# A new order of the head and of all step plans in a fused pooling-attention and mixer kernel

## The chip, the cores and the metric

The kernel runs on one core of a Trainium2 chip. The metric is the device time of one execution, in microseconds, the median of three runs. A run is also profiled; "us" are microseconds from the start of the profiled span.

The core has five engines with a queue of instructions each: TensorE (PE) multiplies matrices, VectorE (DVE), ScalarE (ACT) and GpSimd (POOL) work on elements, SyncE (SP) issues transfers. POOL and ACT issue transfers too. An engine takes its instructions strictly in their order, so an instruction that waits holds up all that stand behind it.

## The reference

Batch 8, 8 heads, 576 rows, head dimension 64; everything comes and goes in float32.

```python
def _attn_ref(q, k, v):
    k_p = k.reshape(B, H, Sp, 8, D).mean(axis=3)      # Sp = 72
    v_p = v.reshape(B, H, Sp, 8, D).mean(axis=3)
    scores = scale * np.matmul(q, k_p.transpose(0, 1, 3, 2))
    attn = softmax(scores)
    return np.matmul(attn, v_p)

x = attn_out.transpose(0, 2, 1, 3).reshape(B, S, H * D)   # 8 x 576 x 512
def _moe_ref(x, w_tok1, w_tok2, w_ch1, w_ch2):
    h = np.maximum(x.transpose(0, 2, 1) @ w_tok1, 0.0) @ w_tok2   # 576 -> 256 -> 576
    u = x + h.transpose(0, 2, 1)
    h2 = np.maximum(u @ w_ch1, 0.0) @ w_ch2                       # 512 -> 1536 -> 512
    return u + h2
```

## The kernel before

**Steps.** The work of a batch is cut into small named steps, each a few instructions on several engines. `2.K0` is step K0 of batch 2. The names that matter here:

- `lk`, `lq`, `lv` (lines 118 to 131): load k, q or v of a batch to bfloat16. POOL issues these transfers; k and v take two each, q takes one. Each landing area has two buffers, so a load waits until the batch two before has been read.
- `K0`, `K1`, `V0`, `V1` (`pool8`, lines 171 to 180): POOL sums groups of eight rows of k or v, half of the heads each, in three additions (lines 174, 175 and 178 or 180). `v1` does the same on DVE. `kpT` (line 222): PE transposes the pooled keys, ACT copies them.
- `Q0`, `Q1` (line 284): DVE transposes the queries. `s0` to `s2` (lines 297 and 306): scores on PE, exponentials on ACT.
- `av0` to `av4` (lines 379 to 384): PE sums the values with their weights, DVE divides. `at0`, `at1` (lines 393, 395): product with w_tok1. `u0` to `u4` (lines 410 to 416): product with w_tok2 on PE, and the sum u = x + h on DVE.
- To give the mixer u with its rows and columns exchanged, batches 1 and 2 use `t0` to `t3` (PE transposes, line 424). From batch 3 on it goes through DRAM: `M0`, `M2`, `M4` write u there (line 434), `M` and `MT` read it back (line 446), both issued by SP, and `T0` to `T5` (line 458) transpose on DVE.

**Units.** The channel mixer of one batch is a unit (`unit_fast`, lines 574 on). Units 0 to 7 are the batches, unit 8 holds the last 64 rows of all batches together. A unit has 24 half tiles of the first product (line 517, ACT writes GT at line 521) and then seven products of 12 matmuls each (line 583), called x, y, z, x again, w, z again and x again; the last unit has no w and two more x. Seven products take the place of eight by sums of GT and of w_ch2 that DVE makes: `=1` to `=4` (lines 545 and 557) and, once, `w0` to `w3`. DVE adds the parts at line 626. A unit yields after each half tile and after every four matmuls of a product, 45 times; these are its slots, 0 to 44, some 0.43 us each.

**The order.** Nothing is scheduled by a program at build time. `HEAD` is the list of steps ahead of unit 0, the loads (`L...`) among them, and `PLAN[n]` says which steps follow which slot of unit n. The steps of batch n+1 and the loads and pooling of batches n+2 and n+3 are woven into unit n in this way. In HEAD, `d4` is four matmuls on zeros, `p0` and `p1` (line 159) permute w_tok2 on ACT and POOL, `kp`, `kt`, `q`, `o`, `e` pool, transpose and score batch 0, `a`, `m`, `X`, `A` are its weighted sums and its token mixer.

Each engine's queue gets the instructions in the order in which the steps stand, and each instruction waits for what it reads and for the buffers that it writes. Some of these waits are not visible in the plan:

- PSUM has four banks that go round (`take` and `give`, lines 81 to 88): a step takes the bank that has been free longest, and its first matmul waits until the bank's last reader is done. Scores and weighted sums share two larger buffers.
- `g` is a gate (lines 711 to 713): DVE sets a flag and POOL copies it, so that POOL's next work does not begin before DVE has come to this place; DVE's next gate waits for POOL's copy.
- At most eight of POOL's transfers are under way: the next one waits for the landing of the one eight before. POOL stands still meanwhile.

In the last unit (`last`), x is kept in two halves, and DVE adds in the order s1, the output addition of y, s5 of z, s of x, and then the outputs.

Of the kernel before, what the change touches and what calls it, by code (L numbers as in the profile page):

```python
# [17 lines left out]
SYNC = mybir.EngineType.SP  # L18


HEAD = """LkA LkT LkB LvT Lq LvA LvB Lt1 Lk1 Lt2 Lc1b Lc1a Lq1 Lc1c Lv1 Lc1d p1 Lc2a Lc2b Lc2c d2 d2 d3 d1 d4 d4 c0 c1 prep q0 kp0 kp1 kt0 q1 d1 o0 kt1 kp2 e0 e1 q3 kt2 o1 q2 e3 vpool0 o3 e2 a00 vpool1 a02 o2 m01 d1 d1 m00 a04 X1 m03 a14 m02 X0 m04 p0 a10 a12 1.kpool m10 m14 m12 m13 m11 A1 A0 X2 X3 A2 A3"""
PLAN = [
# [9 lines left out]
]  # L32


# [1 line left out]
def kernel(  # L36
# [49 lines left out]
    def give(t):  # L86
        i = next(i for i, h in enumerate(held) if h[0] is t)
        free.append(held.pop(i)[1])
# [421 lines left out]
    def chunk(u, c, a):  # L510
        return a[:, c::2] if "paired" in u else a[:, c * P:(c + 1) * P]
# [62 lines left out]
    def unit_fast(n, u):  # L574
        last = n == B
# [4 lines left out]
        def product(ps, a, w, start, after, split=False, end=None):  # L580
            for i in range(2):
                for m in range(NH):
                    nc.tensor.matmul(out=ps[i] if split else ps[:, i], lhsT=chunk(u, i, a(m)), rhs=w(m),  # L583
                                     start=start and m == 0 and (i == 0 or split), stop=(m == NH - 1),
                                     skip_group_check=True)
                    if (i * NH + m) % 4 == 3 and (i, m) != (1, NH - 1):
                        yield
                if split:
                    after(i)
            if not split:  # L590
                after(slice(0, 2))
            if end is not None:
                give(end)
            yield

        def bank(split=False):
            if split:
                return [ps_two.tile([P, 2, 512], FP32, name="p2")[:, 0, 0:256] for _ in range(2)]
            return take([P, 2, 256], FP32)

        def keep(name):
            return outp.tile([P, 2, 256], FP32, name=name, bufs=1)

        def residual(i, half):
            if "paired" in u:
                r = u["u"][:, i].rearrange("p (a k f) e -> p e k a f", a=4, k=4)[:, :, 2 * half:2 * half + 2]
            else:
                r = u["u"][:, i, half * 256:(half + 1) * 256].rearrange("p n e -> p e n")
            return lambda e: r[:, e]

        def cols_of(o, half):
            return lambda e: o[:, e, half * 256:(half + 1) * 256]

        def part(t):
            return (lambda e: t[e]) if type(t) is list else lambda e: t[:, e]

        def plus(out, ps, other, then=None):
            def go(e):
                if type(e) is slice and len(other(e).shape) > 3:
                    go(0)  # L620
                    go(1)
                    return
                aps = [f(e) for f in (out, ps, other)]
                if len(aps[2].shape) == 4:
                    aps[:2] = [x.rearrange("p (k a f) -> p k a f", k=2, a=4) for x in aps[:2]]
                nc.vector.tensor_tensor(out=aps[0], in0=aps[1], in1=aps[2], op=ALU.add)
                if then is not None:
                    then(e)
            return go

        def store_part(cols, engines):
            def go(i):
                if len(engines) == 2:
                    engines[i].dma_start(out=tail_rows(1, cols)[:, i], in_=ob[:, i, cols])
                elif i == 1:
# [4 lines left out]
        oa, ob = (outp.tile([P, 2, DM], FP32, name="o") for _ in range(2))  # L640
        x, y = bank(last), bank()
        s1 = keep("s1")
        yield from product(x, lambda m: GT[:, m, lo], lambda m: w_ch2[:, m, lo], True,
                           plus(part(s1), part(x), residual(0, 0)), last)
        yield from product(y, lambda m: GT[:, NH + m, lo], lambda m: w_ch2[:, NH + m, lo], True,
                           plus(cols_of(oa, 0), part(y), part(s1)), end=y)
        z = bank()
        s5 = keep("s5")
        yield from product(z, lambda m: SG[:, 0, m], lambda m: TW[:, 0, m], True,
                           plus(part(s5), part(z), residual(1, 1)))  # L650
        s2 = keep("s1")
        yield from product(x, lambda m: SG[:, 1, m], lambda m: TW[:, 1, m], False,
                           plus(part(s2), part(x), residual(0, 1)), last)
# [80 lines left out]
    with tc.manual_schedule(engines={PE, POOLE, DVE, ACT, SYNC}):  # L734
# [8 lines left out]
        for i in range(2):  # L743
            nc.vector.memset(values[i][:, :, D], float(POOL))
            nc.vector.memset(exps[i][:, H * S:], 0.0)
            nc.vector.memset(rests[i], 0.0)
        for i, s in enumerate(HEAD.split()):
            if i == 3:
# [34 lines left out]
```

## Time and profile before

| | us |
|---|---|
| median of three runs | 266.19 (266.13 to 266.20) |
| the profiled execution | 266.17 |
| its span | 264.4 |
| TensorE busy | 256.2 |
| VectorE busy | 178.4 |
| ScalarE busy | 119.6 |
| GpSimd busy | 153.1 |

A row of the timeline gives the start in us, the length in us, the engine, the line of the code, the operation, output and inputs with their shapes, and how often it follows itself; in brackets the idle time of the engine before it and what ended that. Rows of the waits give the engine and line that waited, for whom, and in all how long, how often and the longest. Rows of the groups give the total and the mean length in ns. The granted TensorE clock is 0.999 over the span.

### The profile page before, as it was taken

What the parts mean: (1) busy time and instruction counts of PE and PEld (TensorE: products, weight loads), DVE (VectorE), ACT (ScalarE), POOL (GpSimd) and SP (SyncE); (2) the same over time, 40 slices, a digit from 0 to 9 for tenths busy, and PEclk for the clock granted to TensorE, in tenths of its full rate; (3) what the DMA queues carried; (4) which work ended last, traced back from release to release, by engine and by line L of the source; (5) the groups of instructions that cost most, each with busy time, mean ns of one, the idle gap of its engine ahead of it and who ended that gap; (6) DMA issues with size and microseconds to landing.
All of it is one profiled execution on the core that took longest, in us unless ns stands there. A gap on an engine that the chain in (4) does not pass through costs nothing.

```text
span 264.4 us, 5328 instructions
## 1 busy us (share of the span) xinstructions
PE 256.2 (97%) x2121; PEld 160.3 (61%) x2121; DVE 178.4 (67%) x370; ACT 119.6 (45%) x195; POOL 153.1 (58%) x177
## 2 busy tenths in 40 slices
PE   8799999989999999999999999999999999999994
PEld 3685466744677545774487447744874486486483
DVE  3557569996787655895599678844795576184183
ACT  2355763149536456425641575165435412612700
POOL 8577326899999999988959982898200010100000
PEclk9999999999999999999999999999999999999999
DMA  6999999993088928699447940830513053404104
GB/s 141 193 195 206 205 207 208 205 216 80 4 129 141 166 82 171 149 202 266 91 132 107 232 144 17 158 94 4 159 38 122 30 170 80 121 0 102 59 0 159
DMA packets 31704, 34.29 MB, mean 130 GB/s; under 512 B 3136, under 2 KB 23744, under 8 KB 31680
## 3 DMA queue, kind: packets, MB, share of 16 engines
q0 software_dynamic: 17632, 17.64, 42.3%
q1 hardware_dynamic: 13632, 15.93, 20.2%
q10 hardware_dynamic: 416, 0.39, 0.5%
q8 instruction: 16, 0.26, 0.4%
q14 instruction: 8, 0.07, 0.1%
HBM read 38.99 MB, written 12.58 MB: 195 GB/s over the span
## 4 chain that ended last, share of the span: by engine, by line
PE 73%; DVE 12%; POOL 8%; issue 3%; DMA 2%; ACT 1%; POOLq 0%; ACTq 0%
PE p1c L517 10%; PE p1b L517 8%; PE p1a L517 7%; PE p1d L517 7%; PE p1d L583 6%; PE p1c L583 5%; PE p1b L583 4%; PE p1a L583 4%; POOL t L174 3%; PE p L297 3%; DVE x L384 3%; DVE area L545 3%; PE p L379 2%; DMA kr<-in_k_dram 2%; POOL t L175 2%
## 5 line engine op out<-in xcount | busy, mean ns | idle before, releaser
L517 PEld LDWEIGHTS <-w_ch 128*128 128x128 bf16 x432 | 39.5, 98 | 44.4 <-issue 2.7
L713 POOL COPY flag<-flag 1x1 f32<-1x1 f32 x47 | 15.3, 326 | 86.0 <-DVE flag L712 86.0
L583 PEld LDWEIGHTS <-area 128*128 128x128 bf16 x432 | 41.4, 98 | 7.8 <-issue 1.2
L306 ACT ACTIVATE ex<-p 72x768 bf16<-72x768 f32 x42 | 31.6, 803 | 17.1 <-PE p L297 17.1
L583 PEld LDWEIGHTS <-GT 128*128 128x128 bf16 x324 | 30.7, 98 | 7.9 <-issue 1.6
L175 POOL TENSOR_TENSOR t<-t 72x512 f32<-72x512 f32 x23 | 31.2, 1358 | 1.8
L517 PE MATMUL p1c<-uT,w_ch 128*128 128x512 bf16 x116 | 31.4, 379 | 0.0
L521 ACT ACTIVATE GT<-p1b 128x512 bf16<-128x512 f32 x27 | 16.1, 597 | 27.5 <-PE p1b L517 20.9
L521 ACT ACTIVATE GT<-p1c 128x512 bf16<-128x512 f32 x32 | 19.1, 598 | 15.5 <-PE p1c L517 11.7
L517 PE MATMUL p1b<-uT,w_ch 128*128 128x512 bf16 x96 | 26.0, 379 | 0.0
L174 POOL TENSOR_TENSOR t<-kr 72x1024 f32<-72x1024 bf16 x12 | 25.5, 2121 | 0.4
L174 POOL TENSOR_TENSOR t<-vr 72x1024 f32<-72x1024 bf16 x11 | 23.4, 2125 | 1.0 <-DMA vr<-in_v_dram 0.5
L517 PE MATMUL p1a<-uT,w_ch 128*128 128x512 bf16 x88 | 23.9, 379 | 0.0
L517 PE MATMUL p1d<-uT,w_ch 128*128 128x512 bf16 x84 | 22.2, 379 | 0.0
L521 ACT ACTIVATE GT<-p1a 128x512 bf16<-128x512 f32 x25 | 14.9, 597 | 15.4 <-PE p1a L517 14.8
L521 ACT ACTIVATE GT<-p1d 128x512 bf16<-128x512 f32 x24 | 14.4, 599 | 12.8 <-PE p1d L517 7.3
L384 DVE TENSOR_TENSOR x<-p,den 128x512 bf16<-128x512 f32 x28 | 19.3, 691 | 1.0
L545 DVE TENSOR_TENSOR area<-GT 128x1536 bf16<-128x1536 bf16 x9 | 11.3, 1257 | 11.9 <-ACT GT L521 6.7
L557 DVE TENSOR_TENSOR area<-GT 128x1536 bf16<-128x1536 bf16 x9 | 9.5, 1054 | 11.3 <-ACT GT L521 11.3
L379 PEld LDWEIGHTS <-ex 72*128 72x128 bf16 x280 | 12.9, 98 | 6.5 <-DVE x L384 1.4
L379 PE MATMUL p<-vp,ex 72*128 72x65 bf16 x280 | 14.4, 194 | 0.3 <-POOL vp L180 0.2
L118 POOL DMA_DIRECT2D kr<-in_k_dram x17 | 10.9, 646 | 5.6 <-PE p1b L222 1.9
(185 smaller groups left out, 464.2 us busy)
## 6 DMA issues: line engine op xcount, KB each, us to landing
out_dram<-o SPq DMA_DIRECT2D x32, 256.0 KB, 4.2
qb<-in_q_dram POOLq DMA_DIRECT2D x7, 576.0 KB, 9.4
kr<-in_k_dram POOLq DMA_DIRECT2D x7, 512.0 KB, 8.4
vr<-in_v_dram POOLq DMA_DIRECT2D x7, 512.0 KB, 14.0
w_ch<-in_moe_w_ch_dram POOLq DMA_DIRECT2D x5, 512.0 KB, 14.8
mem<-u SPq DMA_DIRECT2D x10, 256.0 KB, 2.2
v<-mem SPq DMA_DIRECT2D x20, 128.0 KB, 2.9
area<-in_q_dram SPq DMA_DIRECT2D x2, 288.0 KB, 3.0
```

Of the source, the lines that this page charges most:

```text
L118: nc.gpsimd.dma_start(out=t[j0:j1, h0:h1].rearrange("j h i d -> j h (i d)"), in_=src[b, h0:h1].rearrange("h (j i) d -> j h (i d)", i=POOL) ...
L174: eng.tensor_tensor(out=t4[:, 0:n], in0=t[:, hs, 0:4], in1=t[:, hs, 4:8], op=ALU.add)
L175: eng.tensor_tensor(out=t4[:, 0:n, 0:2], in0=t4[:, 0:n, 0:2], in1=t4[:, 0:n, 2:4], op=ALU.add)
L306: nc.scalar.activation(out=dst, in_=src, func=AF.Exp, scale=scale)
L379: nc.tensor.matmul(out=ps[:, h // 4, (h % 4) * (D + 1):(h % 4 + 1) * (D + 1)], lhsT=st["ex"][:, h * S + n0:h * S + n0 + P], rhs=st["vp"][: ...
L384: nc.vector.tensor_tensor(out=dst.rearrange("p (a h d) -> p a h d", a=2, d=D), in0=view[:, :, :, 0:D], in1=den[rows, :, :, None].broadcast ...
L517: nc.tensor.matmul(out=ps, lhsT=w_ch1[:, kk, m * P:(m + 1) * P], rhs=uT[kk], start=(kk == 0), stop=(kk == 3))
L521: nc.scalar.activation(out=GT[:, m, :], in_=ps, func=AF.Relu)
L545: nc.vector.tensor_tensor(out=out, in0=a, in1=b, op=ALU.subtract)
L557: nc.vector.tensor_tensor(out=S4[:, 0], in0=GT[:, f, hi], in1=GT[:, sec, hi], op=ALU.add)
L583: nc.tensor.matmul(out=ps[i] if split else ps[:, i], lhsT=chunk(u, i, a(m)), rhs=w(m), start=start and m == 0 and (i == 0 or split), stop= ...
L713: nc.gpsimd.tensor_copy(out=flag[:, 1:2], in_=flag[:, 0:1])
```

## The change

All steps are kept, none is added, and HEAD and every plan are written anew. In `unit_fast`, the output addition of product y is emitted behind the sum s5 of product z if the unit is the last one; y's bank is given back there. The comparison of the two programs shows the same number of matmuls, additions, transfers and gates on each engine. Plans of units 4 to 8 are left out below; in them, of what is spoken of later, 7.Q0 moves from slot 2 to 33 of unit 4, and in unit 6 7.T2 and 7.T0 come to slot 35, ahead of 7.u4.

```diff
-HEAD = """LkA LkT LkB LvT Lq LvA LvB Lt1 Lk1 Lt2 Lc1b Lc1a Lq1 Lc1c Lv1 Lc1d p1 Lc2a Lc2b Lc2c d2 d2 d3 d1 d4 d4 c0 c1 prep q0 kp0 kp1 kt0 q1 d1 o0 kt1 kp2 e0 e1 q3 kt2 o1 q2 e3 vpool0 o3 e2 a00 vpool1 a02 o2 m01 d1 d1 m00 a04 X1 m03 a14 m02 X0 m04 p0 a10 a12 1.kpool m10 m14 m12 m13 m11 A1 A0 X2 X3 A2 A3"""
+HEAD = """LkA LkT LkB Lq LvA LvT LvB Lt1 Lk1 Lt2 Lc1a Lq1 Lc1b Lc1c Lv1 Lc2b Lc1d p1 Lc2a Lc2c d4 c0 prep d3 c1 d4 d2 d1 q0 d2 kp0 kp1 kt0 q1 kt1 o0 kp2 o1 q3 e1 kt2 e0 q2 e3 vpool0 o3 d1 d1 a00 e2 vpool1 o2 a02 m01 d1 a04 m00 a12 m03 X1 m02 a10 m04 X0 p0 a14 1.kpool m11 m12 m14 m13 m10 A1 X3 A0 X2 A2 A3"""
 PLAN = [
-    {0: "2.lk 0.u1 1.kpT 1.Q0 1.Q1", 3: "0.u0 3.lq 2.lq", 6: "1.s0 0.u2", 8: "g", 9: "0.u3 1.s1", 10: "1.vpool1 2.lv", 12: "1.s2 1.vpool0", 13: "=3", 14: "1.av1 1.av2", 17: "1.av0", 18: "1.av4 g", 19: "w0", 20: "3.lv 1.av3", 22: "w1", 23: "g =1 =2", 24: "3.lk", 25: "=4", 26: "1.at0 g", 27: "2.K0", 28: "w3 1.at1", 30: "g", 31: "1.u2", 32: "2.K1", 33: "1.u0 2.V0", 34: "1.u1", 35: "w2", 37: "1.t2", 40: "1.u3", 41: "1.t0", 42: "1.t3", 43: "1.t1 2.Q0 1.u4", 44: "g 2.kpT 2.Q1 3.Q0"},
-    {1: "2.v1 2.s0", 4: "3.K0", 8: "3.K1 2.s2", 11: "g", 12: "2.s1", 15: "3.Q1", 16: "2.av3", 17: "4.lq 2.av1", 18: "4.lk", 19: "2.av0", 20: "2.av4", 23: "2.av2 =1 g", 25: "2.at0 =2", 26: "g", 27: "3.kpT", 28: "2.at1 =4", 31: "2.u3", 32: "3.s2 4.Q1", 33: "2.u2", 34: "5.lk", 35: "3.s0", 36: "3.V1 =3", 37: "2.t3", 39: "3.s1 3.V0 4.lv g 2.u0", 41: "2.u1 2.t2", 42: "2.t0 g", 43: "2.t1 3.av0", 44: "3.av4"},
-    {2: "3.av2", 4: "4.K1", 6: "4.K0 3.av1", 7: "3.av3", 11: "3.at1", 12: "g", 13: "3.at0", 15: "=3", 17: "4.Q0 3.u1 4.kpT", 18: "6.lk 3.u3 4.V1 3.u0", 20: "3.u2 4.s2", 21: "3.u4 3.M0", 23: "4.V0 g", 24: "3.M2", 25: "=1", 26: "5.lq 4.s0", 27: "=2", 28: "g", 29: "=4 6.lq", 30: "4.s1 3.M", 32: "3.T3", 33: "5.lv 3.T0", 35: "g", 36: "4.av1 g", 37: "3.M4 3.T2 3.T1", 38: "6.lv", 40: "g", 41: "3.MT", 43: "4.av2", 44: "4.av4"},
-    {3: "5.K1 4.av0", 5: "4.av3 5.K0", 7: "6.Q0", 8: "4.at1", 10: "4.at0 g", 11: "5.Q1", 12: "5.Q0", 13: "3.T4", 15: "3.T5 5.kpT 4.u3 4.u2 4.u1", 16: "5.V1 g", 17: "5.s0", 18: "=3", 20: "4.u0", 24: "5.s1", 25: "=1 4.M0 4.M2", 26: "=2 =4", 28: "5.V0 5.s2 g", 30: "g", 32: "5.av0 7.lq", 35: "5.av2", 36: "5.av1 4.M", 40: "5.av4 5.av3", 41: "4.T0", 42: "4.T1 4.T3", 43: "4.T2 5.at0 5.at1"},
+    {0: "0.u3 1.Q0 2.lk 1.kpT", 3: "0.u1", 4: "1.s0 g g", 5: "1.Q1", 9: "1.s1 0.u0", 10: "1.vpool1 1.vpool0 g", 11: "1.s2", 12: "=3 0.u2 2.lq", 13: "1.av1", 14: "1.av3", 16: "1.av2", 18: "w0 3.lk", 19: "1.av0 3.lq", 20: "1.av4 w1 g", 23: "1.at1 2.lv", 24: "1.at0 3.lv =1", 25: "=2 =4", 26: "g", 28: "w3", 31: "1.u1 1.u2", 32: "1.t1", 33: "1.t2 w2", 34: "2.K0", 35: "1.u0", 38: "3.Q1 2.K1", 40: "1.u3", 41: "1.t0", 42: "g", 43: "2.Q0 1.t3", 44: "1.u4 2.V0 2.kpT"},
+    {2: "2.s0", 5: "2.Q1", 6: "2.s2", 9: "3.Q0 3.K0", 11: "3.K1", 12: "2.s1", 16: "2.v1", 17: "4.lq 2.av3 g", 18: "2.av2", 19: "2.av4", 22: "2.av1", 23: "2.av0 =1 =3", 24: "=2", 25: "4.lk g", 26: "g =4", 27: "3.kpT 5.lk 2.at0", 28: "g 3.s1 2.at1", 29: "3.V1", 30: "3.s2 2.u2", 32: "2.u3 3.s0", 33: "2.u0", 37: "2.t3", 39: "2.t0", 40: "2.u1 3.V0", 41: "4.Q1 2.t2", 42: "2.t1", 44: "4.lv"},
+    {2: "3.av4", 3: "3.av0 4.K0", 7: "3.av1", 8: "g 4.K1", 10: "3.av2 3.av3", 13: "g 3.at0", 14: "3.at1 g 6.lk", 16: "4.kpT", 17: "=3", 18: "4.Q0 3.u2", 19: "3.u1", 20: "3.u0", 21: "3.M0", 22: "3.u3 4.s2", 23: "3.M2 4.V1 3.u4", 24: "4.V0", 25: "=1", 26: "=2 3.M4", 27: "4.s0 g", 28: "6.lq", 30: "=4 g", 31: "4.s1 5.lv", 34: "3.M g", 35: "4.av2 3.T1", 36: "3.MT", 38: "3.T2", 40: "3.T3 3.T0", 41: "4.av4", 44: "5.lq 3.T5"},
+    {0: "5.K0 5.K1", 1: "4.av1", 4: "g", 6: "6.lv 4.av0", 7: "4.av3 5.Q0", 9: "5.V1 6.Q0", 10: "4.at1 4.at0", 12: "5.kpT", 13: "4.u2", 14: "4.u1", 15: "g", 16: "5.Q1 4.u3", 17: "5.s0", 19: "3.T4 =3", 21: "4.u0", 23: "=1", 25: "5.V0 4.M0", 26: "=2 5.s1", 27: "g", 29: "=4", 30: "5.s2", 31: "g", 33: "5.av2", 35: "5.av0 5.av1 4.M2 4.M", 39: "5.av3", 40: "4.T2 5.av4", 41: "4.T1", 42: "7.lq 4.T3", 43: "5.at0 4.T0", 44: "5.at1"},
...
+        first_out = plus(cols_of(oa, 0), part(y), part(s1))
         yield from product(y, lambda m: GT[:, NH + m, lo], lambda m: w_ch2[:, NH + m, lo], True,
-                           plus(cols_of(oa, 0), part(y), part(s1)), end=y)
+                           (lambda e: None) if last else first_out, end=None if last else y)
         z = bank()
         s5 = keep("s5")
         yield from product(z, lambda m: SG[:, 0, m], lambda m: TW[:, 0, m], True,
                            plus(part(s5), part(z), residual(1, 1)))
+        if last:
+            first_out(slice(0, 2))
+            give(y)
```

10 rows, old and new, of the table PLAN are left out of this document.

## The prediction

> **What bounds the kernel now.** I read the page first, for the share of each engine.
>
> ```profile
> span 264.4 us, 5328 instructions
> ...
> PE 256.2 (97%) x2121; PEld 160.3 (61%) x2121; DVE 178.4 (67%) x370; ACT 119.6 (45%) x195; POOL 153.1 (58%) x177
> ```
>
> TensorE (PE) is the bound, and both kernels issue the same 2121 matmuls. An order can only take away time in which PE waits, or add some. The profiled execution took 266.17 us, 1.8 us more than its span, and the median of the runs is 266.19 us, so one sum serves both. So I read next who keeps PE waiting (columns: total, times, longest, in us).
>
> ```profile
> PE p1c L222 <- POOL kp L178: 0.9, 1, 0.9
> PE p L333 <- ACT ex L322: 0.4, 1, 0.4
> PE p1d L583 <- DVE s L626: 0.3, 1, 0.3
> PE p L379 <- POOL vp L180: 0.2, 1, 0.2
> PE p1b L393 <- DVE x L384: 0.2, 1, 0.2
> ```
>
> Above these rows stand only 1.3 us for the first keys and 1.2 us for the start, in which the changed kernel has nothing new. The view understates each wait by almost 0.2 us, since a matmul's end is modelled: one row's length reaches past the next row's start. Starts tell more. In the timeline of PE (start, length, instruction, idle before) two places show it.
>
> ```profile
> 90.62 0.59 PE L517 MATMUL p1a<-uT,w_ch 128*128 128x512 bf16 x2
> 91.22 0.43 PE L379 MATMUL p<-vp,ex 72*128 72x65 bf16 x8
> 91.49 0.60 PE L517 MATMUL p1a<-uT,w_ch 128*128 128x512 bf16 x2
> 92.18 0.43 PE L379 MATMUL p<-vp,ex 72*128 72x65 bf16 x8
> ...
> 255.01 1.47 PE L583 MATMUL p<-area,area 128*128 128x256 bf16 x12
> 256.78 1.47 PE L583 MATMUL p1d<-w_ch,area 128*128 128x256 bf16 x12 [0.29 <-DVE s L626]
> ```
>
> Twelve matmuls of 256 columns that wait for nothing follow at 0.109 us, 1.31 us in all (1.47 less the modelled overlap), so the last row is 256.78 - 256.32 = 0.46 us late. Two of 512 columns take 0.43 us, so the weighted sums of line 379 at 91.22 and 92.18 are late by 0.17 and 0.26; with 0.12 at 89.05 and 0.37 behind the POOL wait, 0.9 us go between 86 and 93 us. By the same count the other waits are 1.1 us at the transposes of pooled keys (L222, kpT of batch 2), 0.36 at line 393, and in the head 1.1 us in all from 8.04 us on, half of it before line 333. That is 3.9 us: the most that any order can bring.
>
> Where I say below that PE comes to a step at some time, I have laid its matmuls end to end in the new order, from the first keys at 8.04 us on, with the start-to-start times of before (0.216 us for 512 columns, 0.109 for 256, 0.53 for a block of scores), and added the terms found up to there. Times of DVE and POOL follow from these, one operation after the other at the pitch of before.
>
> **The head.** In the changed HEAD the projections by w_tok1 start half a microsecond earlier by my count of matmuls, and the output of the head would come earlier with them, but for one thing. The matmuls of A1 need both halves of w_tok2, which `p1` (POOL) and `p0` (ACT) lay out. p1 now stands behind Lc2b and Lc1d, not behind Lc1d alone.
>
> ```profile
> 19.72 0.80 POOL L163 DMA_DIRECT2D w_ch<-in_moe_w_ch_dram  x1
> 20.49 1.28 POOL L159 COPY w_tok<-area 128x576 bf16<-128x576 bf16 x1
> ...
> 22.42 0.59 PE L476 MATMUL p1c<-w_tok,AT 128*128 128x512 bf16 x2
> ```
>
> One more DMA issue of 0.8 us ahead puts the copy at 21.27 to 22.55 us, and A1 at 22.6 instead of 22.42; PE would be there by 21.9. So the head gains nothing, I take **+0.2 us**. Bounds: -0.5 (another order on POOL at run time, PE sets the start) and +0.4 (the issue stretches by half).
>
> **Unit 0.** Two chains meet here: DVE's sums and POOL's pooling of keys.
>
> ```profile
> 42.57 0.95 DVE L545 TENSOR_TENSOR area<-w_ch,area 128x1536 bf16<-128x1536 bf16 x1
> ...
> 46.30 0.68 DVE L626 TENSOR_TENSOR s<-p1d,u 128x512 f32<-128x512 f32 x1
> 46.91 0.95 DVE L545 TENSOR_TENSOR area<-w_ch,area 128x1536 bf16<-128x1536 bf16 x1
> ```
>
> The weight sum w1 (42.57) waits for the last load of w_ch2, in both kernels the last of the head. Now all five sums of attention stand ahead of it on DVE and w1 can begin about 0.4 us earlier; the three sums of G follow, then s, w3 and the output addition of product y: that one ends near 48.0 us, where it ended at 48.4. But PE now asks for y's PSUM bank earlier: 1.u1 and 1.u2 stand together after slot 31, and the second takes that bank (by the order of takes), near 47.45 us. **+0.55 us**, bounds 0 and 0.7.
>
> ```profile
> 45.00 1.25 POOL L118 DMA_DIRECT2D kr<-in_k_dram  x2 [0.56 <-DMA kr<-in_k_dram]
> 47.08 0.83 POOL L713 COPY flag<-flag 1x1 f32<-1x1 f32 x1 [0.83 <-DVE flag L712]
> ...
> 55.27 1.26 POOL L175 TENSOR_TENSOR t<-t 72x512 f32<-72x512 f32 x1
> 56.61 0.84 POOL L178 TENSOR_TENSOR kp<-t 72x256 bf16<-72x256 f32 x1
> ...
> 59.74 2.13 POOL L175 TENSOR_TENSOR t<-t 72x512 f32<-72x512 f32 x1
> ```
>
> The pooled keys of batch 2 end at 57.45 and PE's transposes wait for them. POOL's queue: two last DMA issues from 45.0 on (each waits for the landing eight issues back, the first 2.lk in both kernels), a gate, 2.K0, a gate, 2.K1. The changed plan has no gate between K0 and K1 (0.9 us), and the gate ahead waits for the s addition that DVE now reaches 0.4 us earlier. So K1 ends near 56.2, and PE, 0.75 us late by the two terms above, arrives near 56.9. The wait goes: **-1.1 us**; if it had to be paid again, 0. The query transpose 3.Q1 is moved up 22 slots, ahead of 1.u3 on DVE, and its load 3.lq is now third in a queue that is full until 60 us: it lands near 53.6 us:
>
> ```profile
> 24.39:55.00 30.61, 30.61 (x260) 19.24 (x259) 24.09 (x43) 14.93 (x25) 16.16 (x19) 1.00 1.22 206
> ```
>
> at the 206 GB/s of this stretch (last column) a load of 0.59 MB takes 2.9 us, and three stand behind 2.lk, which landed just before 45.0. DVE comes there at about 53.7, after s4, so I cost this at nothing; if the load is 1 us later, u3 is, and PE's last transposes have 0.4 us of slack: +0.6.
>
> **Units 1 and 2.** The weighted sums of batch 3 (av0, av4) stood at the end of unit 1, where POOL's pooled values ended at 86.6 us. They now stand after slots 2 and 3 of unit 2, PE near 87.2, and the four others are spread. The 0.9 us go: **-0.9**, bounds -0.9 and -0.4. 4.K1 ends near 96.6, its transposes come at 96.7: nothing, up to +0.6.
>
> **Unit 3** has the new wait that I fear. 5.lq moves from slot 26 of unit 2, ahead of 5.lv, to slot 44, behind it, and 5.Q0 from slot 12 of unit 3 to slot 7.
>
> ```profile
> 109.06 0.75 POOL L128 DMA_DIRECT2D qb<-in_q_dram  x1
> ...
> 110.62 1.28 POOL L118 DMA_DIRECT2D vr<-in_v_dram  x2
> ...
> 124.67 2.12 POOL L174 TENSOR_TENSOR t<-vr 72x1024 f32<-72x1024 bf16 x1 [0.53 <-DMA vr<-in_v_dram]
> ```
>
> Three loads issued from 109.06 on, two of q and one of v, took until 124.6, when POOL could read the last: 15.5 us. The changed order has the same three, q, v, q, and POOL begins them near 108.3. (Its queue: K1 of batch 2 to 56.2; 2.V0 from 57, when its load has landed, to 62; 3.K0 and 3.K1 at 4.45 each to 70.9; loads and gates to 76.9, the last gate behind DVE's sums of G; 3.V1, 3.V0 and a load to 87.4; 4.K0 and 4.K1 to 96.6; gates and a load to 98.7; 4.V1 and 4.V0 with one stretch to 108.3.) So 5.lq, now last, lands near 123.8. DVE comes to 5.Q0 near 118 and stands there. Behind it stand 6.Q0 and the addition of 4.u2, whose bank PE takes for 4.u3 near 125.1 us.
>
> ```profile
> L284 DVE STREAM_TRANSPOSE qD<-qb 128x576 uint32<-128x576 uint32 x14 | 10.3, 758 | 0.1
> ```
>
> Two transposes and an addition at a pitch of some 0.7 us put the bank at 123.8 + 2.1 = 125.9. **+0.8 us**, bounds 0 (landing before 123) and +3.3 (2.5 us later). Beside these loads run SyncE's: 3.M, 3.MT and the stores.
>
> The Trainium skill bears on this. "DMA: Bandwidth & Descriptors", section "Issuing engines are not separate DMA queues", says that transfers of all issuing engines run on the same 16 engines and interleave. By that rule 3.MT, which now goes out before the last q load, shares its time, and the 15.5 us stay. If SyncE's transfers took nothing from POOL's, the three loads would need 8.6 us at the 206 GB/s above, 5.lq would land near 117 and the sum would be -1.7 us. The row at 124.67 speaks for the rule, and the sum keeps its +0.8.
>
> **Unit 3's end.** 0.36 becomes about 0.3, since 4.T2 stands ahead of 5.av4 on DVE: **-0.1**. **Units 4 to 7.** Pooling is 2 us and more ahead of its readers in both; I find only one new pinch, 7.T2 and 7.T0 ahead of 7.u4: **+0.1**, bounds 0 and +0.4.
>
> **The last unit.** DVE's timeline there:
>
> ```profile
> 254.51 0.96 DVE L545 TENSOR_TENSOR area<-GT,area 128x1536 bf16<-128x1536 bf16 x1
> 255.39 0.68 DVE L626 TENSOR_TENSOR o<-p1a,s 128x512 f32<-128x512 f32 x1
> 255.99 0.74 DVE L626 TENSOR_TENSOR s<-p1d,u_tails 128x256 f32<-128x256 f32 x2
> ```
>
> PE's 0.46 us wait is for s (end 256.73), which stands behind the output addition o (pitch 0.6). Moved behind s, o frees it at 256.1, before PE asks at 256.32. What is late next is s of product x at 257.45, asked for at 258.28. **-0.46**, bounds -0.46 and -0.2.
>
> **Sum:** +0.2 + 0.55 - 1.1 - 0.9 + 0.8 - 0.1 + 0.1 - 0.46 = -0.9 us, and 266.17 - 0.9 = 265.3; I say 265.2. The best ends together give -0.5 - 1.1 - 0.9 - 0.36 - 0.46 = -3.3 (262.9).
>
> **Rivals.**
> 1. *The plan does what it says:* no new wait at the bank of y, at 5.Q0 or behind p1. Then -0.9 loses 0.55 + 0.8 + 0.2 and is -2.45: 263.7. For it: pooling and loads have been given room nearly everywhere. Against it: three rows above that I can add up. Chance 0.18.
> 2. *The loads decide, slower:* 5.lq lands after 126, DVE stands still for 8 us and PE waits 3 us at u3 instead of 0.8: +2.2 - 0.9 = +1.3, 267.5. It decides from a landing at 124.7, where the gain is spent; each microsecond beyond costs one. For it: the load has moved behind another of its size, and its reader five slots forward. Against it: POOL may begin the three loads earlier. Chance 0.23.
> 3. *POOL is stretched and the gain is spent:* line 175 took 1.26 us at 55.27 and 2.13 at 59.74. K0 and K1 now run beside w3, w2 and s of unit 0; two such hits put K1's end at 57.9, the wait at kpT returns with 0.9 us, and the time is 266.2. Chance 0.17. (The Trainium skill, "SBUF — State Buffer", section "SBUF: two separate sides", has a rule of this kind: VectorE and GpSimd share one port pair, held for a whole instruction. By that rule these hits come wherever a bf16 sum starts first; the two rows agree, 0.87 us apart.)
>
> **How the numbers follow.** My forecast, 264.4 to 265.6, has 0.42. A measurement of this kernel can tell about 0.2% (0.53 us) from no change: faster means below 265.65, slower above 266.7. Faster: 0.42 + 0.18 and a little of the third, 0.61; same 0.16; slower 0.23. The range reaches into the first rival and past the half of the second: 263.3 to 267.3.
>
> **What would show it.** p1 ending near 22.5 and A1 right behind; K1 of batch 2 ending before 56.5 and kpT's four transposes together; no idle between 86 and 93 us; a DVE wait of about 5 us for qb near 118 to 124; the last product z with no wait. I am wrong if PE waits where none of these stands, or if 5.lq lands before 122.

## The result, and the profile after

| | before | changed |
|---|---|---|
| median of nine runs, us | 266.15 (265.19 to 266.76) | 264.76 (264.03 to 266.43) |
| a second set: before 29 runs, changed 12 | 266.20 | 264.48 (263.60 to 266.32) |
| the profiled execution, us | 266.17 | 264.03 |
| its span, us | 264.4 | 262.2 |

The ratio to the kernel before is 0.9947 (95% interval 0.9926 to 0.9968) in the first set and 0.9941 (0.9922 to 0.9960) in the second: faster by 1.4 to 1.6 us. Below, one execution of no_tail and seven of q5_late, whose granted TensorE clock was 0.986 to 0.994 where all others had 0.997 to 1.000, are left out of the times. The forecast was 265.2, the range 263.3 to 267.3. The execution of the changed kernel that was profiled is the fastest of its nine. So the two traces differ by 2.1 us, 0.5 to 0.7 more than the medians, and what the traces show must be sorted into what the order does and what one execution happened to have.

First the page of the changed kernel. TensorE still is busy nearly all the time, with the same 2121 matmuls; the span is shorter by what it waits less.

```profile
span 262.2 us, 5324 instructions
...
PE 255.8 (98%) x2121; PEld 160.4 (61%) x2121; DVE 179.7 (69%) x370; ACT 119.2 (45%) x195; POOL 150.0 (57%) x177
```

Then the waits of PE (total, times, longest). Of the five rows shown of before none is left; one is new, the bank of u3 in unit 3. Two waits of 0.3 us are not in this view and show only in the starts: one at y's bank, and what is left at kpT (both below).

```profile
PE p1d L232 <- DMA kr<-in_k_dram: 0.9, 1, 0.9
PE p1c L415 <- DVE u L416: 0.4, 1, 0.4
```

Where each unit begins on PE (its first half tile) tells where the time was won. I read these starts from the timelines of PE of both kernels; the last column is worked out from them.

| | before | changed | changed less before |
|---|---|---|---|
| first keys' transposes (L232) | 8.04 | 7.74 | -0.30 |
| unit 0 | 24.60 | 24.18 | -0.42 |
| unit 1 | 57.58 | 56.51 | -1.07 |
| unit 2 | 87.64 | 85.76 | -1.88 |
| unit 3 | 115.70 | 113.51 | -2.19 |
| unit 4 | 145.48 | 143.75 | -1.73 |
| unit 8 | 240.72 | 239.02 | -1.70 |
| span | 264.39 | 262.22 | -2.17 |

Units 0, 1 and 2 win, unit 3 gives half a microsecond back, units 4 to 7 do nothing, and the last unit wins again. Units 1, 2 and 3 are not compared at equal work: in the changed plan 3.av0 and 3.av4 stand in unit 2 and no longer in unit 1, and 4.av1 in unit 3 and no longer in unit 2, each 0.26 us of PE. At equal work units 1 and 2 together win 0.86 us and unit 3 gives back 0.2.

The first wait that the prediction added is at y's bank in unit 0. Two matmuls of 512 columns take 0.43 us, so the second row is 0.73 - 0.43 = 0.30 us late.

```profile
46.83 0.59 PE L415 MATMUL p1b<-AT,w_tok 128*128 128x512 bf16 x2
47.56 0.59 PE L415 MATMUL p1d<-AT,w_tok 128*128 128x512 bf16 x2
```

The chain of POOL in unit 0 (timeline of POOL; in brackets its idle time and what ended it):

```profile
46.11 0.83 POOL L717 COPY flag<-flag 1x1 f32<-1x1 f32 x1 [0.29 <-DVE flag L716]
46.91 2.12 POOL L174 TENSOR_TENSOR t<-kr 72x1024 f32<-72x1024 bf16 x1
49.11 1.27 POOL L175 TENSOR_TENSOR t<-t 72x512 f32<-72x512 f32 x1
50.45 1.44 POOL L178 TENSOR_TENSOR kp<-t 72x256 bf16<-72x256 f32 x1
51.97 2.13 POOL L174 TENSOR_TENSOR t<-kr 72x1024 f32<-72x1024 bf16 x1
...
55.54 0.84 POOL L178 TENSOR_TENSOR kp<-t 72x256 bf16<-72x256 f32 x1
```

K0 and K1 of batch 2 follow each other without a gate, and K1 ends at 56.38, where it ended at 57.45. PE has come to the transposes at 56.1, so 0.3 us of the wait are left: four transposes take 0.13 us when nothing holds them, here 0.44.

```profile
56.07 0.61 PE L222 MATMUL p1d<-ident,kp 72*128 72x72 bf16 x4
56.51 1.03 PE L517 MATMUL p1b<-uT,w_ch 128*128 128x512 bf16 x4
```

In unit 3 DVE and PE show the new wait:

```profile
118.34 0.69 DVE L384 TENSOR_TENSOR x<-p,den 128x512 bf16<-128x512 f32 x1
123.30 1.44 DVE L284 STREAM_TRANSPOSE qD<-qb 128x576 uint32<-128x576 uint32 x2 [4.26 <-DMA qb<-in_q_dram]
124.66 0.69 DVE L416 TENSOR_TENSOR u<-p1c,x 128x512 bf16<-128x512 f32 x1
```

```profile
124.36 0.59 PE L517 MATMUL p1b<-uT,w_ch 128*128 128x512 bf16 x2
125.40 0.59 PE L415 MATMUL p1c<-AT,w_tok 128*128 128x512 bf16 x2 [0.45 <-DVE u L416]
```

DVE stands still for 4.26 us before 5.Q0 and 6.Q0, because 5.lq lands at 123.27. Behind the two transposes stands the addition of u2, and only then does PE get the bank for u3: two matmuls of 512 columns take 0.43 us, so the row at 125.40 is 1.04 - 0.43 = 0.61 us late. In the last unit the products of 12 matmuls now follow each other at 1.31 us:

```profile
253.31 1.47 PE L583 MATMUL p<-area,area 128*128 128x256 bf16 x12
254.62 1.47 PE L583 MATMUL p1a<-w_ch,area 128*128 128x256 bf16 x12
255.93 1.47 PE L583 MATMUL p<-area,area 128*128 128x256 bf16 x12
```

### The profile page after: what moved, and what is told of

Read it like the earlier page. It is cut to its first block, busy times and chain, and to the rows that moved or that the text cites. A ratio compares the mean times of both kernels' runs of the same rounds, so it can differ in the third digit from the quotient of the medians.

```text
span 262.2 us, 5324 instructions
## 1 busy us (share of the span) xinstructions
PE 255.8 (98%) x2121; PEld 160.4 (61%) x2121; DVE 179.7 (69%) x370; ACT 119.2 (45%) x195; POOL 150.0 (57%) x177
## 4 chain that ended last, share of the span: by engine, by line
PE 80%; POOL 8%; DMA 7%; DVE 3%; issue 1%; POOLq 0%
PE p1d L517 9%; PE p1c L517 9%; PE p1a L517 8%; PE p1b L517 7%; PE p1b L583 7%; PE p1c L583 7%; PE p1a L583 6%; DMA qb<-in_q_dram 5%; PE p1d L583 4%; PE p L297 3%; PE p L379 3%; POOL t L174 2%; POOL t L175 2%; DMA kr<-in_k_dram 2%; PE p L583 2%; PE p1d L393 2%
## 5 line engine op out<-in xcount | busy, mean ns | idle before, releaser
L717 POOL COPY flag<-flag 1x1 f32<-1x1 f32 x47 | 12.6, 269 | 94.5 <-DVE flag L716 94.5
L521 ACT ACTIVATE GT<-p1d 128x512 bf16<-128x512 f32 x29 | 17.3, 597 | 27.0 <-PE p1d L517 21.4
L517 PE MATMUL p1d<-uT,w_ch 128*128 128x512 bf16 x104 | 28.8, 379 | 0.0
L517 PE MATMUL p1c<-uT,w_ch 128*128 128x512 bf16 x96 | 26.1, 379 | 0.0
L517 PE MATMUL p1a<-uT,w_ch 128*128 128x512 bf16 x92 | 25.3, 379 | 0.0
L517 PE MATMUL p1b<-uT,w_ch 128*128 128x512 bf16 x92 | 24.2, 379 | 0.0
L174 POOL TENSOR_TENSOR t<-vr 72x1024 f32<-72x1024 bf16 x11 | 24.1, 2187 | 0.3
L521 ACT ACTIVATE GT<-p1a 128x512 bf16<-128x512 f32 x26 | 15.5, 596 | 11.8 <-PE p1a L517 9.2
L521 ACT ACTIVATE GT<-p1c 128x512 bf16<-128x512 f32 x27 | 16.1, 598 | 8.7 <-PE p1c L517 8.3
L583 PE MATMUL p1c<-area,area 128*128 128x256 bf16 x120 | 15.4, 273 | 0.0
```

The lines of the kernel that those rows point to most:

```text
L174: eng.tensor_tensor(out=t4[:, 0:n], in0=t[:, hs, 0:4], in1=t[:, hs, 4:8], op=ALU.add)
L517: nc.tensor.matmul(out=ps, lhsT=w_ch1[:, kk, m * P:(m + 1) * P], rhs=uT[kk], start=(kk == 0), stop=(kk == 3))
L521: nc.scalar.activation(out=GT[:, m, :], in_=ps, func=AF.Relu)
L717: nc.gpsimd.tensor_copy(out=flag[:, 1:2], in_=flag[:, 0:1])
```

## The experiments

Theory A is the one behind the prediction: the time is a sum of PE's single waits, and a wait that goes shortens the kernel by its length. Rival B says that a wait that is taken away comes back at the next reader of the same data, or that the gain has another source (the head, chance). All times below are medians; each kernel ran between runs of the kernel before. The changed kernel itself ran again beside no_tail, old_head and q5_first only (the kernel before took 266.20 us there); q0_later, best2, before_k01 and before_av ran beside 266.07 us of the kernel before, before_av2, gate_back, q5_late and best3 beside 266.36. The kernel before itself moved by 0.3 us between these, so a difference of that size from the changed kernel says nothing there.

**The changed kernel again**, unaltered.

> The changed kernel once more, unaltered, as the base for the other three. Its first profile took 264.03 us, the lowest of its nine times; the median was 264.76. If the difference between executions lies in the landing of loads (the first keys, 5.lq), a second profile shows the same PE waits with other lengths there and none elsewhere: first keys 7.7 to 8.5 us, the wait of u3 in unit 3 anywhere from 0.3 to 1.5 us, and a median of 264.5 to 265.0. If it lies in the order itself (an engine that now and then comes late), waits stand at other places than in the first profile.

It took 264.48 us. The profiled execution (264.77) has the first keys at 7.73, as before, and the wait of u3 with 0.66 us. Two losses stand where the first profile has none. One is at PE's transposes of the values of batch 1 (line 264), for the load of v.

```profile
31.18 0.59 PE L517 MATMUL p1a<-uT,w_ch 128*128 128x512 bf16 x2
32.06 1.03 PE L264 MATMUL p1c<-vr,ident 72*72 72x256 bf16 x8 [0.28 <-DMA vr<-in_v_dram]
```

The second row is 0.88 - 0.43 = 0.45 us late. The other follows from 3.lq, which the prediction had at no cost: DVE waits 0.60 us for it before 3.Q1, 1.u3 comes behind that on DVE, the transposes 1.t3 start 0.28 us late on PE, and at kpT, where PE comes later by as much, nothing is left.

```profile
54.14 0.78 DVE L284 STREAM_TRANSPOSE qD<-qb 128x576 uint32<-128x576 uint32 x1 [0.60 <-DMA qb<-in_q_dram]
```

So executions of one program differ by where a load lands, by up to half a microsecond at a place, and the first profile had good luck there.

**The tail without its change.**

```diff
-                           (lambda e: None) if last else first_out, end=None if last else y)
+                           first_out, end=y)
...
-        if last:
-            first_out(slice(0, 2))
-            give(y)
```

> The changed HEAD and plans with the last unit as before (the output addition of y ahead of s5). Theory A, the gain is a sum of PE's single waits: the wait before the last product z comes back with 0.36 to 0.46 us and nothing else changes, so the time is 0.4 us above the changed kernel's. Rival B, the end of the kernel is set by the output transfers or by DVE's last additions, and the wait was covered: no change, within 0.1 us.

264.84 us (0.9951, 0.9934 to 0.9967), 0.4 above the changed kernel, with intervals that overlap. The times alone do not settle it; the trace shows that the wait is back, at 254.76 - 252.94 - 1.31 = 0.51 us.

```profile
252.94 1.47 PE L583 MATMUL p<-area,area 128*128 128x256 bf16 x12
254.76 1.47 PE L583 MATMUL p1a<-w_ch,area 128*128 128x256 bf16 x12 [0.34 <-DVE s L626]
```

**The head of before** under the changed plans (only the HEAD line exchanged).

> The changed plans and last unit with the HEAD of before. By the two profiles unit 0 began at 24.60 before and 24.18 after, of which 0.30 is the first keys' transposes (8.04 and 7.74 us). Theory A, as my prediction had it: the new head is worth nothing or costs 0.2 us, and the 0.4 us are chance of one execution: within 0.2 us of the changed kernel. Rival B, the new head is a part of the gain (the wait before line 333 fell from 0.47 to 0.16 us): 0.3 to 0.5 us slower than the changed kernel.

264.29 us (six runs; 0.9925, 0.9898 to 0.9951): no slower than the changed kernel's 264.48. The new head is worth nothing that can be measured. Most of the 0.42 us at the start of unit 0 belong to the one execution. The first keys are transposed from 7.36 to 8.33 us on in the nine profiles with the new head (the middle one 7.74), from 7.78 to 8.39 in the five with the old one (8.06), so their load may land 0.3 us earlier, which so few do not show; but from there to unit 0 the old head takes 16.55 to 16.56 us in all five, the new one 16.44 to 17.46, because in some executions PE then waits for p1 or for q of batch 0. Unit 0 begins between 24.18 and 25.12 with the new head, between 24.34 and 24.95 with the old.

**The load of q ahead of v again.**

```diff
-28: "6.lq", 30: "=4 g", 31: "4.s1 5.lv", ... 44: "5.lq 3.T5"
+28: "6.lq", 30: "=4 g", 31: "4.s1 5.lq 5.lv", ... 44: "3.T5"
```

> The changed kernel with 5.lq moved back ahead of 5.lv (slot 31 of unit 2 in place of slot 44). Theory A: 5.lq lands near 119.5 in place of 123.3, DVE's 4.3 us wait at 5.Q0 shrinks to 1 us or less, PE's 0.61 us before u3 goes, and the time is 0.6 us below the changed kernel's. Rival B: the three loads share the same time, 5.lv lands at 123.3 or later, POOL waits some 1.3 us for it before 5.V1, and the delay comes back on PE at the weighted sums of batch 5 (136 us on) or is spent at another bank: no change, or 0.3 us.

265.77 us (0.9979, 0.9962 to 0.9996): 1.3 us slower than the changed kernel, and rival B by more than it said. PE's wait for u3 has gone, but v of batch 5 now lands at 125.5 in place of 119.6, and POOL stands still for it:

```profile
121.33 1.28 POOL L118 DMA_DIRECT2D vr<-in_v_dram  x2
125.67 2.12 POOL L174 TENSOR_TENSOR t<-vr 72x1024 f32<-72x1024 bf16 x1 [3.06 <-DMA vr<-in_v_dram]
```

POOL's additions now run beside DVE's sums of G. The first of these (line 557) takes 2.81 us, where it took 1.37 from 130.74 on in the changed kernel:

```profile
130.74 2.81 DVE L557 TENSOR_TENSOR area<-GT 128x1536 bf16<-128x1536 bf16 x1 [0.83 <-ACT GT L521]
```

DVE's whole queue is late by that, and PE pays at 133.6, at 136.2 and most of all at the weighted sums of batch 5 at 138.7.

```profile
137.28 0.42 PE L379 MATMUL p<-vp,ex 72*128 72x65 bf16 x8
138.72 0.43 PE L379 MATMUL p<-vp,ex 72*128 72x65 bf16 x8 [1.01 <-DVE x L384]
```

So the changed plan's late 5.lq, which I had counted as a pure loss, is a trade: 0.6 us at u3 against 1.9 from 133 to 139 us (0.58 at a product that waits for a sum of G, then 0.14 and 1.17 at weighted sums).

**The load of q later still**: in unit 3 `0: "5.K0 5.K1"` becomes `0: "5.K0 5.lq 5.K1"`, and 5.lq goes from slot 44 of unit 2.

> The changed kernel with 5.lq moved further back, behind 5.K0 (slot 0 of unit 3): 4.3 us later on POOL. In four executions of the changed order 5.lq landed 8.95, 9.76, 9.82 and 10.03 us after unit 3's start and PE waited 0, 0.61, 0.66 and 0.88 us before u3. Theory A: one us of landing beyond 9.15 us is one us of PE; landing at 124.5 to 126 (beside SyncE's stores, issued at 113.8 to 116.5) gives a wait of 1.8 to 3.3 us and a time 1.2 to 2.7 us above the changed kernel's. Rival B: the 16 engines are shared, the load lands no more than 0.5 us later, and so does the end.

266.15 us (five executions, 265.07 to 266.73, the profiled one the longest), 1.7 us above the changed kernel. The load lands at 126.01, and the view of PE's waits shows 2.6 us where the changed kernel has 0.4 (both understate by 0.2):

```profile
PE p1c L415 <- DVE u L416: 2.6, 1, 2.6
```

Five executions of this place, from the timelines of DMA, DVE and PE:

| execution | 5.lq lands, us after unit 3's start | PE late at u3, us |
|---|---|---|
| no_tail | 8.95 | 0 |
| the changed kernel, first profile | 9.76 | 0.61 |
| the changed kernel again | 9.82 | 0.66 |
| old_head | 10.03 | 0.88 |
| q5_late | 11.94 | 2.77 |

From 9.16 us on each microsecond of landing is a microsecond of PE. Theory A holds here; Rival B, a landing at most 0.5 us later, does not.

**The reader moved in place of the load.** Loads as in the changed plan; in unit 3:

```diff
-7: "4.av3 5.Q0", 9: "5.V1 6.Q0", ... 14: "4.u1", 15: "g", 16: "5.Q1 4.u3", 17: "5.s0", 19: "3.T4 =3"
+7: "4.av3", 9: "5.V1", ... 14: "4.u1 5.Q0", 15: "g", 16: "5.Q1 4.u3", 18: "6.Q0", 19: "3.T4 =3 5.s0"
```

> The changed kernel with the order of loads left alone, but 5.Q0 moved from slot 7 of unit 3 to slot 14 (behind 4.u2 and 4.u1 on DVE), 6.Q0 from 9 to 18 and 5.s0 from 17 to 19. Theory A: DVE no longer stands still in front of 4.u2 until 5.lq lands near 123.5, PE's 0.61 to 0.66 us before u3 go, and nothing comes back, since no load is moved: 0.6 us below the changed kernel (264.5 to 264.8). Rival B: the scores of batch 5 (5.s0) now wait for 5.Q0 and 5.Q1: 0.2 us or nothing gained.

263.84 us (six runs, 263.26 to 264.36; 0.9907, 0.9885 to 0.9929), 0.6 below the changed kernel; against the kernel before beside it 2.2. In this execution 5.lq landed as late as 125.54, and PE does not notice: the additions of u2 and u1 stand ahead of the transposes, and PE goes from one pair of matmuls to the next at 0.43 us.

```profile
124.00 0.73 DVE L416 TENSOR_TENSOR u<-p1c,x 128x512 bf16<-128x512 f32 x1 [4.24 <-PE p1c L415]
124.86 0.73 DVE L416 TENSOR_TENSOR u<-p1a,x 128x512 bf16<-128x512 f32 x1
125.56 1.49 DVE L284 STREAM_TRANSPOSE qD<-qb 128x576 uint32<-128x576 uint32 x2
```

```profile
125.09 0.59 PE L517 MATMUL p1b<-uT,w_ch 128*128 128x512 bf16 x2
125.53 0.59 PE L415 MATMUL p1c<-AT,w_tok 128*128 128x512 bf16 x2
```

**One gate, from both sides.** In the kernel before, the gate between 2.K0 and 2.K1 moves behind K1 (`30: "g"` goes, `32: "2.K1"` becomes `32: "2.K1 g"`); in the changed kernel a gate is put between them (`37: "g"` is added).

> The kernel before with one gate moved: the one between 2.K0 and 2.K1 (slot 30 of unit 0) now stands behind 2.K1. Theory A (PE's single waits add up): the gate's 0.9 us on POOL go, K1 ends near 56.6 in place of 57.45, PE's wait at kpT falls from 1.07 us to 0.2, and the time is 0.85 us below the kernel before. Rival B: without the gate K1's additions meet DVE's sums w3 and w2, are stretched by 0.6 to 0.9 us each, and the wait stays: no change within 0.2 us.

> The changed kernel with a gate put back between 2.K0 and 2.K1 (slot 37 of unit 0). My prediction gave the missing gate 0.9 us of the 1.1 at kpT. Theory A, as predicted: the copy waits on POOL for some 0.9 us beside DVE's w2, K1 ends near 57.3 in place of 56.4, PE's wait at kpT grows from 0.29 to 1.1 us and the time by 0.8. Rival B, as before_k01 has it (K1's first addition took 2.73 us without the gate): the gate takes little or no time, since DVE's w2 is over when POOL comes to it in the changed plan, and the time grows by 0.2 us or nothing; the gain at kpT then came from K0's earlier start (46.9 in place of 47.9).

The changed kernel with the gate took 265.38 us (0.9959, 0.9943 to 0.9976), 0.6 to 0.9 more than without; PE's wait at kpT grew from 0.3 to 0.95 us. Theory A, at 0.65 us where I had given the gate 0.9: from the start of K0 to the end of K1 POOL takes 10.12 us, without the gate 9.47. POOL waits at it for DVE, which has the sum w2 and three additions ahead of the flag:

```profile
51.45 1.44 POOL L178 TENSOR_TENSOR kp<-t 72x256 bf16<-72x256 f32 x1
53.51 0.17 POOL L717 COPY flag<-flag 1x1 f32<-1x1 f32 x1 [0.63 <-DVE flag L716]
53.65 2.11 POOL L174 TENSOR_TENSOR t<-kr 72x1024 f32<-72x1024 bf16 x1
```

The kernel before without its gate took 266.29 us beside 266.07 (1.0005, 0.9986 to 1.0025): nothing gained. K1's first addition, which begins while DVE runs w2 (a bf16 sum, 51.19 to 52.81), took 2.73 us in place of 2.12, and the wait at kpT is still there with 0.95 us.

```profile
52.07 2.73 POOL L174 TENSOR_TENSOR t<-kr 72x1024 f32<-72x1024 bf16 x1
54.88 1.27 POOL L175 TENSOR_TENSOR t<-t 72x512 f32<-72x512 f32 x1
56.23 0.84 POOL L178 TENSOR_TENSOR kp<-t 72x256 bf16<-72x256 f32 x1
```

DVE's w2 beside it, and below that w2 of the changed kernel:

```profile
51.19 1.62 DVE L545 TENSOR_TENSOR area<-w_ch 128x1536 bf16<-128x1536 bf16 x1
...
49.41 1.78 DVE L545 TENSOR_TENSOR area<-w_ch 128x1536 bf16<-128x1536 bf16 x1
```

So K1 ended 0.4 us earlier, PE came 0.3 earlier in this execution, and little is left. The Trainium skill, "SBUF — State Buffer", section "SBUF: two separate sides", has VectorE and GpSimd share one port pair that one of them holds for a whole instruction; the 0.61 us that the addition grew beside w2 agree with it, and the gate had kept the two apart at about the same price (0.82 us between K0 and K1, without it 0.07). In the changed plan K1 begins at 51.97, when w2 (49.41 to 51.19) is over, and its three additions take 2.13, 1.28 and 0.84 us. So leaving out the gate paid in the order whose w2 comes earlier and not in the one where K1 meets it; no run moves w2 alone.

**The weighted sums of batch 3 alone**, in the kernel before (3.av4 and 3.av0 to slots 2 and 3 of unit 2, 3.av1 to 7, 3.av2 and 3.av3 to 10), and then with the products that read them (3.at0 to slot 13, 3.at1 to 14).

> The kernel before with the weighted sums of batch 3 alone placed as in the changed plan: 3.av4 and 3.av0 after slots 2 and 3 of unit 2 (they stood at the end of unit 1), 3.av1 after 7, 3.av2 and 3.av3 after 10. Theory A: PE's 0.81 us between 86 and 93 us go and the time is 0.8 us below the kernel before. Rival B: the sums end later on DVE, the products by w_tok1 (3.at1 after slot 11) wait for them, and half or all of it is paid there: 0 to 0.4 us below.

> The edit of before_av with the reader moved too: 3.at0 and 3.at1 stand after slots 13 and 14 of unit 2, as in the changed plan (they stood at 13 and 11). In before_av the products of line 393 waited 0.28 and 0.62 us at 93.7 to 94.2 for the sums that had been moved. Theory A, a wait goes only when the whole chain from pooled values to product is moved: the 0.9 us at line 393 go, those between 88 and 92 us stay away, and the time is 0.6 to 0.9 us below the kernel before. Rival B: DVE's gate ahead of the sums (2.21 us behind a copy on POOL in before_av) keeps the sums late wherever the reader stands: within 0.3 us of the kernel before.

266.64 us (1.0018, 1.0000 to 1.0036) and 266.95 us (1.0017, 1.0000 to 1.0033): neither is faster. With the sums alone the waits between 88 and 92 us went, and the product behind them was late by 0.28 and 0.62 us (the second shown here as 0.46 of idle time):

```profile
93.65 0.87 PE L393 MATMUL p1d<-x,w_tok 128*128 128x512 bf16 x2
94.98 0.38 PE L393 MATMUL p1d<-x,w_tok 128*128 128x512 bf16 x1 [0.46 <-DVE flag L712]
```

With the products moved too that wait is gone as well, and units 1 and 2 together took 57.59 us from start to start in place of 58.12: 0.5 of the 0.9 us. The rest went into a new wait at the first matmul of unit 2, since the sums had stood between the last transposes of u and the half tile that reads them.

```profile
PE p1b L517 <- ACT uT L425: 0.2, 1, 0.2
```

That matmul is 0.40 us late. The half microsecond was then lost again in unit 3 (31.32 us, before 29.78), in three waits at weighted sums. The first, 0.54 us at 118.79, belongs to batch 4: PE had come 0.3 us earlier than in the kernel before, but DVE's additions there stood 0.4 us later (118.05 in place of 117.66). The other two, 0.40 and 0.68 us, follow v of batch 5, which landed at 126.3 in place of 124.5; whether the edit made that load late or this execution did is not settled. Theory A as I had used it, one edit and its wait, falls here; rival B named the wrong engine for it (DVE's gate did not hold the products up once they were moved).

**More waits taken away at once.** best2 is q0_later with three edits in unit 0 (below), best3 is q0_later with 1.u1, 1.u2, 1.t1, 1.t2 and w2 a slot later.

```diff
-10: "1.vpool1 1.vpool0 g", 11: "1.s2", ... 31: "1.u1 1.u2", 32: "1.t1", 33: "1.t2 w2", 34: "2.K0", ... 44: "1.u4 2.V0 2.kpT"
+10: "g", 11: "1.s2 1.vpool1 1.vpool0", ... 31: "1.u1", 32: "1.u2", 33: "1.t1 w2", 34: "1.t2 2.K0", ... 44: "1.u4 2.V0"
...
-{2: "2.s0", 5: "2.Q1"
+{0: "2.kpT", 3: "2.s0", 5: "2.Q1"
```

> The edit of q0_later and three more in unit 0 of the changed kernel: 1.u2 a slot behind 1.u1 (their transposes a slot later), 2.kpT after slot 0 of unit 1 with 2.s0 a slot later, and 1.vpool1 and 1.vpool0 a slot later, behind 1.s2. Theory A: besides the 0.6 us of q0_later the waits for y's bank (0.20), at kpT (0.29) and at line 264 (0 to 0.44, where v of batch 1 landed late) go: 1.1 us or a little more below the changed kernel, 263.3 to 263.6. Rival B: each wait only moves to the next reader of the same chain (t1, 2.s0, 1.av1), and the time is that of q0_later within 0.2 us.

> q0_later with 1.u1, 1.u2, 1.t1, 1.t2 and w2 of unit 0 all a slot later (0.43 us). Theory A: y's bank is free when 1.u2 asks, and the 0.2 to 0.4 us of PE there go: 0.2 to 0.4 us below q0_later (263.84). Rival B: w2 and the sums behind it end later on DVE or stretch 2.K0, and kpT's wait of 0.28 us grows by as much: equal to q0_later.

264.41 us (0.9924, 0.9902 to 0.9946) and 264.30 us (0.9919, 0.9900 to 0.9938): no better than q0_later. Rival B: the wait at y's bank went in both, and the transposes behind it came 0.3 us late (at 50.84 and 49.88 us); in best2 the scores of batch 2 took 0.3 us longer at 61.23 where the transposes of keys had waited. In both executions q of batch 0 landed late as well (the rows are of best2; in best3 the second has 0.3), which it did in none of the other seven profiles with this head:

```profile
PE p1d L232 <- DMA kr<-in_k_dram: 1.0, 1, 1.0
PE p1b L275 <- DMA qb<-in_q_dram: 0.6, 1, 0.6
```

q0_later is the fastest kernel of the study; its interval against the kernel before just overlaps that of the changed kernel.

## Why the prediction was right, step by step

| term | predicted, us | first profile | in other executions of the changed order |
|---|---|---|---|
| head | +0.2 | -0.42, of it -0.30 first keys | about 0 (old_head against the changed kernel) |
| bank of y in unit 0 | +0.55 | +0.30 | 0.29 to 0.60 |
| kpT of batch 2 | -1.1 | -0.78 | 0.29 to 0.32 us are left, in one execution none (0.28 lost just before) |
| weighted sums of batch 3 | -0.9 | -0.92 | the same |
| 5.lq at u3 | +0.8 | +0.61 | 0 to 0.88 |
| at of unit 3 | -0.1 | -0.36 | the same |
| units 4 to 7 | +0.1 | 0 | 0 |
| last unit | -0.46 | -0.46 | the same |
| sum | -0.9 | -2.0 | about -1.6 |

Each wait is worked out from the starts on PE, as in the prediction; what is left to the 2.17 us of the spans are pieces of 0.1 us and less. The last sum takes 0 for the head, 0.3 for y's bank and 0.65 for 5.lq; the medians say -1.4 to -1.7. Six of the eight signs are right, and the other two terms are zero. The forecast of 265.2 was too dark by 0.4 to 0.7 us. The waits stood where it put them, but for the head; the sizes were off in several small terms, which partly cancel. **The head:** p1 does stand one DMA issue later (20.82 to 22.10 us, predicted 21.27 to 22.55), and PE waits for it in some executions (0.3 us in the views of no_tail and best3), not in the first profile; the wait before line 333, 0.4 us in before's view of the waits, has no row in the changed kernel's. **y's bank:** the output addition ended at 47.5, not 48.0; DVE was half a microsecond ahead of my count, since the weight sum w1 began at 41.48 and not 42.2. **at of unit 3** went whole: I had put 4.T2 in front of it on DVE and it cost nothing. **kpT** was the one that I had too bright: K1 ended at 56.4 where I had 56.2, and PE came at 56.1, not 56.9, since the two delays that should have made it late were smaller.

The wait that I feared most came as forecast: 5.lq landed at 123.27 (forecast 123.8), DVE stood still for 4.26 us (about 5) and PE lost 0.61 us (0.8). The nearness is in part luck: POOL began the three loads at 108.83 and not 108.3, they took 14.4 us and not 15.5, and in other executions of this order PE lost between 0 and 0.88 us. The second rival's point is right as well: q5_late shows a microsecond for a microsecond, and the profiled order stayed on the good side of it. The first rival (263.7) missed that wait; q0_later, which takes it away, came to 263.84, though with 0.4 us at y's bank that the rival left out. The third, POOL stretched beside DVE, happened once in K0 (1.44 in place of 0.84 us, beside w2) and not in K1; in before_k01, an order that the change does not have, it ate the gain as described. The prediction's own row for it, line 175 at 59.74, stood beside DVE's pooling of v (line 174, from 59.21 to 60.73) and not beside one of the sums that it feared; the meeting with such a sum is what before_k01 shows. PE also waited where no term stood: 0.45 us at line 264 in the second profile, 0.3 and 0.7 at scores of batch 1 in those of q0_later and gate_back. These come and go between executions of the same steps.

One step of the reasoning was weaker than its number. I costed the edits one by one, as if each owned its wait. The runs on the kernel before show that this gate alone and these sums alone bring nothing to the median. In the changed order the gate is worth 0.65 us, together with a w2 that comes earlier. The sums' 0.9 us need the products moved with them, which brings 0.5 up to unit 3; that the last 0.4 needs the transposes of u moved away from their reader is read from one trace and not tested.

## What to carry to other kernels

In a program whose queues are fixed at build time, cost a reordering by chains: follow the moved step to its reader and to what used to fill the gap, and count a wait as gone only where that reader has room. When a load is late, moving another load up hands the delay to whoever shares the transfers; moving the reader behind work that does not need the load cost nothing here. The profiles of this kernel carried half a microsecond of luck in its loads, so check the terms of a sum against a second one.

## What the runs showed of the hardware

The same load in the same order landed between 8.95 and 11.29 us after its unit's start (the last in q0_later: 125.54 against 114.25), a spread of 2.3 us. In q0_later, where PE does not wait for that load, six executions spread over 1.1 us, the changed kernel's twelve over 2.7; that the landing accounts for the difference is likely and not shown. What stands ahead among the loads takes the shared time: with q ahead of v, q landed 3.3 us earlier (119.93 in place of 123.27) and v 5.9 us later (125.51 in place of 119.62); counted from the start of unit 3, 4.0 earlier and 5.3 later, more than that spread. The Trainium skill, "DMA: Bandwidth & Descriptors", section "Issuing engines are not separate DMA queues", says that transfers interleave on shared engines; the trace agrees. In q5_late a load issued 4.9 us later (115.98 in place of 111.08) landed 2.7 us later, in one execution each, which the spread alone could nearly give.

Work on GpSimd and bf16 sums on VectorE stretched each other by large pieces where they met: an addition went from 2.12 to 2.73 us, another from 0.84 to 1.44, the copy of one flag from 0.17 to 0.83, and a sum of DVE from 1.37 to 2.81. A plan that lets them meet can lose more than the wait that it was made to remove.
